# Threshold attention before two feed-forward layers on one core: weight conversions issued one at a time, and a pair's value products in four parts

## The chip, the cores and the metric

The kernel runs on one core of one Trainium2 chip. Its time is the device time of one launch in microseconds (us). A core has TensorE (PE in the profile, with its weight loads as PEld), VectorE (DVE), ScalarE (ACT), GpSimd (POOL), and SyncE (SP), which here issues the transfers between HBM and SBUF. Each engine works through its own list of instructions in order; a semaphore holds an instruction until what it needs on another engine is done.

## The reference

Attention over 4 x 8 heads of 576 rows and 64 columns, in which a row keeps only the scores within `tau` of its maximum, and then two feed-forward layers (512 to 1536 to 512 and 512 to 2048 to 512) over all 2304 tokens, in float32:

```python
scores = q @ k.T / sqrt(64)                     # per head, 576 x 576
scores = where(scores >= max(scores) - tau, scores, -1e9)
attn = exp(scores - max(scores)); attn /= sum(attn) + 1e-9
x = concat_heads(attn @ v)                      # 2304 x 512
x = (sigmoid(x @ w_gate) * (x @ w_val)) @ w_out
out = g(x @ w2_in) @ w2_out                     # g: piecewise quadratic
```

The weights reach the kernel as 64-bit floats, so the kernel has to turn them into float32 itself.

## The kernel before, in words

**Attention** goes over 16 pairs of heads (`p`), each in 5 steps (`u` = 0 to 4), 80 steps in all, numbered `t` = 5p + u. Below u0 to u4 are these steps. A step of u0 to u3 takes 128 query rows of both heads; u4 takes the 64 rows left over of each head, together in one tile. In a step four things happen that belong to different rows, as a pipeline written out by hand in the loop over `t` (L392 to L454):

- TensorE: `scores` of step t (L252, at u4 L248) into the PSUM tiles `wa` and `wb`; `turns` of step t-2 (L295 transposes the masked weights into PSUM tile `wt`, first those of one head and then of the other, and L296 transposes the left-over columns `lt`); a part of the products with the values (`attend`, L319) of the pair before.
- VectorE: `maxima` of step t (L261, one per head, reading `wa` and `wb`), then `masks` of step t-1 (L281, one per head; at u4 there is one row tile, so one of each).
- ScalarE: `copies` of step t-2 (L301 and L305, out of `wt` and `left`), `exponents` of step t (L273), `drain` (L329), which takes the value products out of the PSUM tile `av`.
- GpSimd: thresholds (L264), the copy of left-over columns `lt` behind each mask pair (L288), and the division by the row sums (L350).

`wa`, `wb`, `wt`, `left` and `av` exist once each, so the scores of the next step wait for the maxima of this one, and the transposes of one step for ScalarE's copies of the one before.

The value products of a pair are two rounds (`r` = 0, 1) of five column blocks `c` = 0 to 4; the table `rounds` (L386) says at which step which blocks are done. Block 4 uses the left-over columns (`rl`). `drain` follows in the step that does block 4.

**Work put into the attention steps.** `background` (L352) turns the first six weight blocks (groups `g`) into float32 while attention runs. A group is a transfer (`load_w`, L129), one ScalarE operation (`extract`, L145) and six VectorE operations (`convert`: L155, L157, L159, L161, L165, L169). The kernel takes one piece of it with `next(bg)`: at u0 of the pairs 1 to 12, ahead of the masks (L420), where a piece is three VectorE operations, and at u2 of the even pairs (L441), where it is the extract. Over the last three pairs the same place at u0 yields `"gap"` (L424) to the loop in `ffn` (L807), which then issues the VectorE halves of all `begun` splits into a high and a low float32r part (`split_xs`, L477, 768 columns; `split_list`, L192, 512 columns): two, two and three at one time. Their ScalarE halves are issued at the end of u4 before.

After attention the first layer starts with weight transfers, conversions and products of its own (`hidden`, `conversions`), all issued in program order behind the last attention steps.

Of the kernel before, what the change touches and what calls it, by code (L numbers as in the profile page):

```python
# [29 lines left out]
def kernel(  # L30
# [57 lines left out]
    high0 = const.tile([P, KD * P], F32, name="high0")  # L88
# [7 lines left out]
    w32 = {(0, 0, 0): ring[0], (0, 0, 1): ring[1]}  # L96
# [12 lines left out]
    def run(*gens):  # L109
        for g in gens:  # L110
            for _ in g:
                pass

    def load_w(ph, g):

        f, i = divmod(g, 3 - ph)
        ins, wo = ((w_gate, w_val), w_out) if ph == 0 else ((w2_in,), w2_out)
        if i < len(ins):
            src = ins[i][:, 2 * f * P : 2 * (f + 1) * P].rearrange("(k p) f -> p k f", p=P)
        else:  # L120
            src = wo[f * P : (f + 1) * P, :].rearrange("p (k f) -> p k f", k=KD)
        if ph == 0 and g < 6:
            t = early_raw[g % 2]
        else:
            n = 2 * KD * P
            t = pools["words"][:, pools["n"] % 6 * n :][:, :n]
            pools["n"] += 1
        r = t.bitcast(U32)
        nc.sync.dma_start(out=r.rearrange("p (k f) -> p k f", k=KD), in_=src)  # L129
        raws[ph, g] = r.rearrange("p (f w) -> p f w", w=2)  # L130
# [10 lines left out]
    def extract(ph, gs, c):  # L141

        n = KD * P
        for i, g in enumerate(gs):
            nc.scalar.activation(  # L145
                c[:, i * n : (i + 1) * n], raws[ph, g][:, :, 1].bitcast(F32), AF.Copy, scale=2.0**-112
            )

    def convert(ph, gs, c, a):


        n = KD * P
        c, a = c[:, : len(gs) * n], a[:, : len(gs) * n]
        cu, au = c.bitcast(U32), a.bitcast(U32)
        nc.vector.tensor_scalar(c, c, -DBL_TOP, DBL_TOP, op0=ALU.max, op1=ALU.min)  # L155
        yield
        nc.vector.tensor_scalar(au, cu, 3, None, op0=ALU.logical_shift_left)  # L157
        yield
        nc.vector.scalar_tensor_tensor(au, cu, 0x80000000, au, op0=ALU.bitwise_and, op1=ALU.bitwise_or)  # L159
        yield  # L160
        nc.vector.tensor_scalar(cu, au, 0xFF800000, None, op0=ALU.bitwise_and)  # L161
        yield
        for i, g in enumerate(gs):
            ci = c[:, i * n : (i + 1) * n]
            nc.vector.scalar_tensor_tensor(  # L165
                ci, raws.pop((ph, g))[:, :, 0], 2.0**-52, ci, op0=ALU.mult, op1=ALU.mult
            )
            yield
        nc.vector.tensor_tensor(a, a, c, op=ALU.add)  # L169
        yield  # L170
# [29 lines left out]
    def attention():  # L200
# [14 lines left out]
        U = nf + 1  # L215
        N = NP * U
# [73 lines left out]
        def turns(p, u):  # L290
            pr = pt.pop((p, u))
            for e in range(1 if u == nf else 2):
                for c in range(nf):
                    cs = slice(c * P, c * P + P)
                    nc.tensor.transpose(wt[:, e, cs], pr[:, e, cs], ident)  # L295
            nc.tensor.transpose(left[:, :P], lts.pop((p, u)).rearrange("p a b -> p (a b)"), ident)  # L296
# [34 lines left out]
        def denom(p):  # L331
            rs = sums[p % 2]
            nc.vector.reciprocal(rs, rs)
# [14 lines left out]
        def normalise(p, s):  # L348
            x, c = x_of(p), slice(s * HS, s * HS + HS)
            nc.gpsimd.tensor_tensor(x[:, c], x[:, c], rbs[:, p % 2 * S :][:, c], op=ALU.mult)  # L350

        def background():  # L352

            for g in range(2):
                load_w(0, g)
            yield
            for g in range(6):
                extract(0, (g,), high0)
                yield
                n = KD * P  # L360
                ops = convert(0, (g,), high0, w32[0, 0, g // 3][:, g % 3 * n : (g % 3 + 1) * n])
                run(itertools.islice(ops, 3))
                yield
                run(ops)
                if g + 2 < 6:
                    load_w(0, g + 2)
                yield

        def warm(n):

# [11 lines left out]
        warm(10)  # L382
        corner(0)
        bg = background()

        rounds = {5: (0, 0, 2), 6: (0, 2, 5), 7: (1, 0, 2), 8: (1, 2, 4), 9: (1, 4, 5)}  # L386
        final = {5: (0, 0, 5), 7: (1, 0, 5)}
        parts = {}
        for p in range(NP):
# [2 lines left out]
        for t in range(N + 9):  # L392
            p, u = divmod(t, U)
            on = t < N
            mk = divmod(t - 1, U) if 1 <= t <= N else None
            at = divmod(t - 2, U) if 2 <= t <= N + 1 else None

            pd, ud = divmod(t - U, U)
            pd2, ud2 = divmod(t - 2 * U, U)
            if ud2 in (2, 3) and 0 <= pd2 < NP:  # L400
                normalise(pd2, ud2 - 2)
            if on:
                scores(p, u)
            if t == N + 1:
                yield t - N, True
            if at:
                turns(*at)
            if ud == 2 and 0 <= pd < NP:
                nc.tensor.transpose(left[: 2 * nf + 1, P : 2 * P], sums[pd % 2], ident)
            for part in parts.get(t, ()):  # L410
                attend(*part)
            if on:
                maxima(p, u)
            if at:
                copies(*at)
            if on:
                exponents(p, u)
            if ud == 1 and 0 <= pd < NP:
                denom(pd)
            if on and u == 0 and p > 0:  # L420
                if p < 13:
                    next(bg, None)
                else:
                    yield t - N, "gap"  # L424
            if ud == 2 and 0 <= pd < NP:
                sum_rows(pd)
            for part in parts.get(t, ()):
                if part[2][-1] == nf:
                    drain(*part[:2])
            if mk:  # L430
                masks(*mk)
                if mk[1] == nf:
                    nc.gpsimd.tensor_scalar(sums[mk[0] % 2], sums[mk[0] % 2], 1e-9, None, op0=ALU.add)
            if on:
                if u == 1 and p + 1 < NP:
                    corner(p + 1)
                if u == 2 and p + 2 < NP:
                    load(p + 2)
                if u == 4 and p + 2 < NP:
                    load_v(p + 2)  # L440
                if t == 1 or u == 2 and p % 2 == 0 and p < 12:  # L441
                    next(bg, None)
            if ud == 3 and 0 <= pd < NP:
                spread(pd)
            if t == N - 1:
                wides[:] = [wb, wa, wt]
            if t == N:
                run(bg)
                nc.scalar.activation(dummy, half, AF.Sigmoid)
                st1.close()  # L450
            if t == N + 2:
                st2.close()
                ps_o.close()
            yield t - N, False  # L454

    def ffn(att):


        with ExitStack() as st:
# [340 lines left out]
                            up(0, 0, 0, n, i, pv[i], [kk])  # L800
                        yield

            early, taken, xops = {}, [], {}
            more = first_up()
            ahead = [split_xs(0, 0, 0, T, [c]) for c in range(KD)] + split_list(0, 0, 0, False)
            second = iter(())
            for step, free in att:  # L807
                if free == "gap":
                    for g in begun:
                        run(g)  # L810
                    continue
                if free:
                    late = sb("late", 1)
                    wins.append(late.tile([P, 4 * KD * P], F32R, name="win_1"))
                    wouts.extend(late.tile([P, 2, DM], F32R, name=f"wout_{i}") for i in (1, 2))
                    hp_ = sb("hp_", 2)
                    pools["words"] = cv("words", 1).tile([P, 12 * KD * P], F32, name="words")
                    pools["n"] = 0
                    for _, _, gs in todo[:2]:
                        for g in gs:  # L820
                            load_w(0, g)
                    continue
                if step in (-16, -11, -6):
                    begun, ahead = (ahead[:2], ahead[2:]) if step < -6 else (ahead, [])
                    for g in begun:
                        next(g)
                if step == 1:
                    second = split_parts(0, 0, 1, False)
                if step >= 0:
                    run(itertools.islice(second, 2))  # L830
                    run(itertools.islice(more, {0: 4, 1: 2, 2: 2}.get(step, 0)))
# [7 lines left out]
            n = 2 * KD * P  # L839
            slots = [wmore[:, i * n : (i + 1) * n] for i in range(4)] + [x[:, :n] for x in ring]  # L840
            n = 3 * KD * P
# [7 lines left out]
            for s in range(NS):  # L849
                nxt = order[s + 1] if s + 1 < NS else None  # L850
                ops = 8 if order[s][1] == 0 else 6
# [25 lines left out]
                _, t, f = order[s - 1]  # L877
# [74 lines left out]
```

## Time and profile before

| | us |
|---|---|
| median of three runs | 1143.96 |
| lowest and highest run | 1143.52, 1143.96 |
| the profiled execution, its own time | 1143.82 |
| its span, from the first to the last instruction | 1142.0 |
| TensorE busy in the span | 1109.9 (97%) |
| VectorE busy | 849.0 (74%) |
| ScalarE busy | 620.9 (54%) |
| GpSimd busy | 138.1 (12%) |

All durations below are from that one execution. Attention takes about the first 288 us of its span. A TensorE record ends by a model, and neighbouring records overlap by some hundredths of a us; where "idle before" stands behind a row, the engine did nothing in that time, and the name behind the arrow is what ended last before it went on.

### The profile page before, as it was taken

How to read it: one execution, taken by the hardware profiler on the slowest of the kernel's cores; microseconds unless marked ns; L12 is line 12 of the kernel's file. 1: busy time of each engine (PE TensorE's matmuls, PEld its weight loads, DVE VectorE, ACT ScalarE, POOL GpSimd, SP SyncE). 2: the span in 40 equal slices, each digit the busy share in tenths (PEclk: the TensorE clock that was granted, in tenths of full speed). 3: DMA queues.
4: the chain of work that ended last, by engine and by line, in shares of the span. 5: the costliest groups of instructions: out<-in, count | busy, mean ns of one | idle time of the engine just before them, and what ended most of it. 6: DMA issues, size and time to landing. Idle time of an engine off the chain costs nothing.

```text
span 1142.0 us, 17341 instructions
## 1 busy us (share of the span) xinstructions
PE 1109.9 (97%) x6372; PEld 944.5 (83%) x6372; DVE 849.0 (74%) x1484; ACT 620.9 (54%) x1048; POOL 138.1 (12%) x315
## 2 busy tenths in 40 slices
PE   8999999999799999999999999989999999999998
PEld 5555656556699999999999999988888888988887
DVE  6888888888499999767777762576677767676663
ACT  5777777787444344333344322366566655656553
POOL 3444544555100000000000000000000000000000
PEclk9999999999999999999999999999999999999999
DMA  4323233220665566455446524032312432143301
GB/s 131 88 76 89 78 81 78 62 71 21 212 205 177 176 199 231 168 183 178 154 161 212 176 78 162 19 111 86 133 67 104 156 121 97 72 161 114 111 20 55
DMA packets 65141, 139.09 MB, mean 122 GB/s; under 512 B 9616, under 2 KB 35872, under 8 KB 65056
## 3 DMA queue, kind: packets, MB, share of 16 engines
q1 hardware_dynamic: 64912, 137.98, 36.1%
q8 instruction: 50, 0.82, 0.3%
q14 instruction: 35, 0.29, 0.1%
q10 hardware_dynamic: 144, 0.00, 0.0%
HBM read 111.15 MB, written 26.81 MB: 121 GB/s over the span
## 4 chain that ended last, share of the span: by engine, by line
PE 85%; DVE 8%; ACT 3%; issue 2%; DMA 1%; SPq 0%; POOL 0%; DVEq 0%; POOLq 0%; ACTq 0%
PE y L743 15%; PE pu L610 14%; PE y L761 13%; PE pgv L486 8%; PE pgv L485 8%; PE pgv L487 8%; PE av L319 6%; PE w L295 5%; PE w L252 5%; DVE s L261 2%; PE w L248 2%; DVE p L281 1%; DVE high L165 1%; ACT sqs L619 1%; ACT sqs L620 1%
## 5 line engine op out<-in xcount | busy, mean ns | idle before, releaser
L485 PE MATMUL pgv<-xflat,win 128*128 128x384 f32 x560 | 188.5, 337 | 5.9 <-ACT act L541 3.8
L486 PE MATMUL pgv<-xflat,win 128*128 128x384 f32 x560 | 188.4, 336 | 0.1
L743 PE MATMUL y<-wout,hh 128*128 128x512 f32 x576 | 185.4, 397 | 3.0 <-ACT hh L628 3.0
L487 PE MATMUL pgv<-xflat,win 128*128 128x384 f32 x560 | 188.3, 336 | 0.0
L761 PE MATMUL y<-hh,wout 128*128 128x512 f32 (+1 forms) x576 | 146.7, 337 | 0.0
L261 DVE TENSOR_SCALAR_CACHE_REDUCE s<-w,nscale 128x576 f32<-128x576 f32 x144 | 112.7, 816 | 33.6 <-PE w L252 23.8
L743 PEld LDWEIGHTS y<-wout,hh 128*128 128x128 f32 x576 | 108.9, 189 | 28.0 <-ACT hh L628 3.3
L545 DVE TENSOR_TENSOR act<-pgv,act 128x384 f32<-128x384 f32 x70 | 38.9, 556 | 104.2 <-PE pgv L487 103.9
L743 PE MATMUL y<-wout,hl 128*128 128x512 f32 x288 | 114.3, 397 | 0.5 <-DVE hl L629 0.5
L485 PEld LDWEIGHTS pgv<-xflat,win 128*128 128x128 f32 x560 | 105.9, 189 | 7.9 <-ACT act L541 4.1
L281 DVE SCALAR_TENSOR_TENSOR p<-s,mx,ex 128x576 f32<-128x576 f32 x144 | 112.1, 812 | 0.5 <-POOL lt L288 0.5
L541 ACT ACTIVATE act<-pgv 128x384 f32<-128x384 f32 x70 | 34.2, 489 | 137.1 <-PE pgv L487 136.8
L273 ACT ACTIVATE ex<-s,mx 128x576 f32<-128x576 f32 x144 | 104.8, 775 | 7.2 <-DVE s L261 6.8
L486 PEld LDWEIGHTS pgv<-xflat,win 128*128 128x128 f32 x560 | 106.0, 189 | 2.0 <-DVE xflat L477 0.4
L761 PEld LDWEIGHTS y<-hh,wout 128*128 128x128 f32 x576 | 98.1, 188 | 11.3
L610 PE MATMUL pu<-xflat,win 128*128 128x384 f32 x576 | 105.1, 337 | 1.0 <-DVE sqs L689 0.7
L487 PEld LDWEIGHTS pgv<-xflat,win 128*128 128x128 f32 x560 | 106.0, 189 | 0.0
L546 ACT ACTIVATE hh<-act 128x384 fp32r<-128x384 f32 x72 | 38.0, 527 | 121.7 <-DVE act L545 121.3
L610 PEld LDWEIGHTS pu<-xflat,win 128*128 128x128 f32 x576 | 100.6, 188 | 2.4 <-DVE sqs L689 1.4
L295 PEld LDWEIGHTS w<-ident,p 128*128 128x128 f32 x576 | 62.8, 141 | 41.6 <-ACT ex L273 36.6
L761 PE MATMUL y<-hl,wout 128*128 128x512 f32 (+1 forms) x288 | 97.1, 337 | 0.0
L301 ACT ACTIVATE r<-w 128x1024 f32<-128x1024 f32 x64 | 65.7, 1026 | 49.7 <-PE w L295 49.6
(140 smaller groups left out, 1928.6 us busy)
## 6 DMA issues: line engine op xcount, KB each, us to landing
wmore<-saved SPq DMA_DIRECT2D x32, 512.0 KB
words<-in_moe_w_out_dram SPq DMA_DIRECT2D x26, 512.0 KB
tsum<-tsaved SPq DMA_DIRECT2D x24, 512.0 KB
wmore<-saved SPq DMA_DIRECT2D x15, 768.0 KB
words<-in_moe_w_in_dram SPq DMA_DIRECT2D x16, 512.0 KB
saved<-w SPq DMA_DIRECT2D x16, 512.0 KB
w<-saved SPq DMA_DIRECT2D x16, 512.0 KB
w<-saved SPq DMA_DIRECT2D x9, 768.0 KB
```

Source lines behind the costliest of these rows:

```text
L261: nc.vector.tensor_scalar(t[:, e], w[:, :, :HS], nscale, None, op0=ALU.mult, op1=ALU.min, accum_out=mx[:, 0, e : e + 1])
L273: nc.scalar.activation(ex[:, e], t[:, e], AF.Exp, scale=-1.0, bias=mx[:, 0, e : e + 1])
L281: nc.vector.scalar_tensor_tensor(pr[:, e], t[:, e].rearrange("p a b -> p (a b)"), mx[:, 1, e : e + 1], ex[:, e].rearrange("p a b -> p (a b ...
L295: nc.tensor.transpose(wt[:, e, cs], pr[:, e, cs], ident)
L301: nc.scalar.activation(rt[r].rearrange("p e c n -> p (e c) n")[:, :, o : o + P], wt.rearrange("p e (c n) -> p (e c) n", n=P), AF.Copy,)
L319: nc.tensor.matmul(av[e * D : e * D + D, :n], vs[p % 3][:, e, c], rt[r][:, e, c] if c < nf else rl[r], start=c == 0, stop=c == nf,)
L485: nc.tensor.matmul(ps, ih[:, i, kk], xh[:, kk, c], start=(kk == 0), stop=False)
L486: nc.tensor.matmul(ps, ih[:, i, kk], xl[:, kk, c], start=False, stop=False)
L487: nc.tensor.matmul(ps, il[:, i, kk], xh[:, kk, c], start=False, stop=(kk == KD - 1))
L610: nc.tensor.matmul(ps[bank], l[:, k], r[:, k], start=bool(new) and k == m == 0, stop=k == HK - 1 and m == 2, skip_group_check=True,)
L743: nc.tensor.matmul(y[b], l[:, ts_], r, start=first and m == 0, stop=last and m == 2)
L761: nc.tensor.matmul(at(y, a, b), l[:, ds_], r[:, c], start=new and m == 0, stop=last and m == 2, skip_group_check=True,)
```

## The change

Three edits. The six operations of `convert` become six pieces, taken one at a time behind the masks at u0, u2 and u3 of each pair, from step 3 to step 62; the place at u0 ahead of the masks goes. (The extra piece at u2 of even pairs stays, so there a VectorE operation and an extract come together.) From step 63 on the same three places yield `"gap"`, which now issues one split instead of all. And the last block of the second round of value products moves from u4 to u3, its `drain` with it.

```diff
-                ops = convert(0, (g,), high0, w32[0, 0, g // 3][:, g % 3 * n : (g % 3 + 1) * n])
-                run(itertools.islice(ops, 3))
-                yield
-                run(ops)
+                yield from convert(0, (g,), high0, w32[0, 0, g // 3][:, g % 3 * n : (g % 3 + 1) * n])
                 if g + 2 < 6:
                     load_w(0, g + 2)
-                yield
...
-        rounds = {5: (0, 0, 2), 6: (0, 2, 5), 7: (1, 0, 2), 8: (1, 2, 4), 9: (1, 4, 5)}
+        rounds = {5: (0, 0, 2), 6: (0, 2, 5), 7: (1, 0, 2), 8: (1, 2, 5)}
...
-            if on and u == 0 and p > 0:
-                if p < 13:
-                    next(bg, None)
-                else:
-                    yield t - N, "gap"
...
                 masks(*mk)
...
+            if on and u in (0, 2, 3) and t > 2:
+                if t <= 12 * U + 2:
+                    next(bg, None)
+                else:
+                    yield t - N, "gap"
...
                 if free == "gap":
-                    for g in begun:
-                        run(g)
+                    run(*begun[:1])
+                    del begun[:1]
                     continue
```

On TensorE, from u3 of a pair over u4 to u0 of the next (`w_126` and `w_127` are `wa` and `wb`, `w_128` is `wt`):

```order
 L319 MATMUL av<-r_161,v_164 64x320 x4
+L319 MATMUL av<-rl_163,v_164 64x320 x2
 L248 MATMUL w_126<-qk,corner_75 128x288 x2
 L295 MATMUL w_128<-ident,p 128x128 x8
 L296 MATMUL left<-ident,lt 128x128
-L319 MATMUL av<-rl_163,v_164 64x320 x2
 L252 MATMUL w_126<-qk 128x288
 L252 MATMUL w_127<-qk 128x288
```

Two products (four records in the trace) moved from behind u4's transposes to ahead of its scores, so that nothing stands between those transposes and the scores of the next pair.

On VectorE, the end of a pair and u0 of the next, before (`s` and `mx` are the outputs of the maxima, `p` of the masks, `high_84` and `w_0_82` the tiles of a conversion):

```order
L261 TENSOR_SCALAR s,mx_77<-w_126,nscale 128x576
L281 SCALAR_TENSOR_TENSOR p,sum_81<-s,mx_76,ex 128x576 x2
L261 TENSOR_SCALAR s,mx_76<-w_126,nscale 128x576
L261 TENSOR_SCALAR s,mx_76<-w_127,nscale 128x576
L161 TENSOR_SCALAR high_84<-w_0_82 128x512
L165 SCALAR_TENSOR_TENSOR high_84<-raw_86,high_84 128x512
L169 TENSOR_TENSOR w_0_82<-w_0_82,high_84 128x512
L281 SCALAR_TENSOR_TENSOR p,sum_81<-s,mx_77,ex 128x576
```

Three operations of a conversion stand between u0's maxima and the one mask of u4.

The same engine with the change, from u2's masks of an even pair to u0 of the next:

```order
L281 SCALAR_TENSOR_TENSOR p,sum_80<-s,mx_77,ex 128x576 x2
L169 TENSOR_TENSOR w_0_82<-w_0_82,high_84 128x512
L261 TENSOR_SCALAR s,mx_77<-w_126,nscale 128x576
L261 TENSOR_SCALAR s,mx_77<-w_127,nscale 128x576
L281 SCALAR_TENSOR_TENSOR p,sum_80<-s,mx_76,ex 128x576 x2
L155 TENSOR_SCALAR high_84<-high_84 128x512
L261 TENSOR_SCALAR s,mx_76<-w_126,nscale 128x576
L281 SCALAR_TENSOR_TENSOR p,sum_80<-s,mx_77,ex 128x576 x2
L261 TENSOR_SCALAR s,mx_77<-w_126,nscale 128x576
L261 TENSOR_SCALAR s,mx_77<-w_127,nscale 128x576
L281 SCALAR_TENSOR_TENSOR p,sum_80<-s,mx_76,ex 128x576
L157 TENSOR_SCALAR w_0_82<-high_84 128x512
```

One operation now stands behind the masks at u2, u3 and u0, none at u4 and u1, and u4's mask comes right behind u0's maxima.

## Rows read from the trace of the kernel before

**Rows 1.** From 100 to 150 us: PE, PEld, DVE, ACT, POOL busy; clock, DMA share, GB/s.

```profile
100.00:150.00 50.00, 47.41 (x336) 29.48 (x336) 44.03 (x114) 36.47 (x69) 23.66 (x53) 1.00 0.35 92
```

**Rows 2.** Waits of TensorE's products, 20 to 285 us: total us, times, longest us.

```profile
PE w L295 <- DVE p L281: 10.1, 12, 1.0
PE w L295 <- ACT ex L273: 2.8, 3, 1.0
```

**Rows 3.** Timeline (start us, us, instruction, [idle before]): TensorE, u0 to next u0.

```profile
125.77 1.24 PE L252 MATMUL w<-qk 64*128 64x288 f32 x8
...
129.09 1.24 PE L252 MATMUL w<-qk 64*128 64x288 f32 x8
131.02 0.63 PE L295 MATMUL w<-ident,p 128*128 128x128 f32 x4 [0.68 <-DVE p L281]
...
133.13 1.24 PE L252 MATMUL w<-qk 64*128 64x288 f32 x8
...
136.77 1.24 PE L252 MATMUL w<-qk 64*128 64x288 f32 x8
...
140.30 1.24 PE L248 MATMUL w<-qk,corner 128*128 128x288 f32 x4
141.38 1.04 PE L295 MATMUL w<-ident,p 128*128 128x128 f32 x8
...
142.45 0.76 PE L319 MATMUL av<-rl,v 128*64 128x320 f32 x4
143.14 1.24 PE L252 MATMUL w<-qk 64*128 64x288 f32 x8
144.31 1.09 PE L295 MATMUL w<-ident,p 128*128 128x128 f32 x8
```

**Rows 4.** Timeline of VectorE over the same pair: u0 and u1, then u4.

```profile
128.53 0.42 DVE L155 TENSOR_SCALAR high<-high 128x512 f32<-128x512 f32 x1
...
129.44 0.69 DVE L159 SCALAR_TENSOR_TENSOR w<-high,w 128x512 uint32<-128x512 uint32 x1
130.05 0.81 DVE L281 SCALAR_TENSOR_TENSOR p<-s,mx,ex 128x576 f32<-128x576 f32 x1
...
131.00 0.82 DVE L261 TENSOR_SCALAR_CACHE_REDUCE s<-w,nscale 128x576 f32<-128x576 f32 x1
...
141.58 0.82 DVE L261 TENSOR_SCALAR_CACHE_REDUCE s<-w,nscale 128x576 f32<-128x576 f32 x1 [0.49 <-PE w L248]
...
142.32 0.81 DVE L281 SCALAR_TENSOR_TENSOR p<-s,mx,ex 128x576 f32<-128x576 f32 x1
```

**Rows 5.** The two splits of one gap in the last pairs, VectorE.

```profile
251.15 1.82 DVE L477 TENSOR_TENSOR xflat<-xall,xflat 128x768 fp32r<-128x768 f32 x2
```

**Rows 6.** Pair 0, u4 and the next u0: masks, transposes, maxima, scores.

```profile
18.63 0.81 DVE L281 SCALAR_TENSOR_TENSOR p<-s,mx,ex 128x576 f32<-128x576 f32 x1
18.83 0.42 PEld L295 LDWEIGHTS w<-ident,p 128*128 128x128 f32 x4 [0.76 <-ACT rl L305]
...
19.51 0.42 PEld L295 LDWEIGHTS w<-ident,p 128*128 128x128 f32 x4 [0.26 <-DVE p L281]
19.58 0.82 DVE L261 TENSOR_SCALAR_CACHE_REDUCE s<-w,nscale 128x576 f32<-128x576 f32 x1
...
20.46 1.24 PE L252 MATMUL w<-qk 64*128 64x288 f32 x8 [0.19 <-DVE s L261]
```

**Rows 7.** The last u4 and the step behind it: ScalarE's copy, then TensorE's transposes.

```profile
282.94 1.03 ACT L301 ACTIVATE r<-w 128x1024 f32<-128x1024 f32 x1 [0.86 <-PE w L295]
284.02 1.09 PE L295 MATMUL w<-ident,p 128*128 128x128 f32 x8 [0.32 <-ACT r L301]
```

**Rows 8.** GpSimd at u1: two thresholds, the second beside a mask, then the left-over copy.

```profile
131.99 0.28 POOL L264 TENSOR_SCALAR mx<-mx,tau_b 128x1 f32<-128x1 f32 x1 [0.35 <-DVE s L261]
132.66 0.85 POOL L264 TENSOR_SCALAR mx<-mx,tau_b 128x1 f32<-128x1 f32 x1 [0.38 <-DVE s L261]
...
134.25 0.29 POOL L288 COPY lt<-p 128x128 f32<-128x128 f32 x1 [0.73 <-DVE p L281]
```

More of the change, by code (lines that the diff above doesn't have):

```diff
@@ L801, in first_up @@
                         yield
-            early, taken, xops = {}, [], {}
+            early, taken, xops, begun = {}, [], {}, []
             more = first_up()
```

## The prediction

> **What bounds the kernel now.** I read the busy shares first, by stretch. Over most of attention TensorE works 47.41 of 50 us and VectorE 44.03, at a granted clock of 1.00 [rows 1]. So TensorE sets the pace, some 5% of its time is idle, and VectorE has little to spare. The clock is at its upper level (2.4 GHz) with these idles in it, so their removal gives none back.
>
> Next, the waits of TensorE's products: they are nearly all one wait, the transposes L295 for the masks L281, 12 times and 10.1 us in all, and three more of 2.8 us put down to ScalarE [rows 2]. That is 12.9 us in 15 places, one a pair.
>
> Then the timeline of one pair, to see where. From one first score product to the next, u0 takes 3.32 us, u1 4.04, u2 3.64, u3 3.53 and u4 2.84 [rows 3]: 17.37 us a pair. The wait lies in u1, here 0.68 us. VectorE shows why: at u0 three conversion operations run from 128.53 to 130.05, ahead of the one mask of u4, which ends at 130.86 [rows 4]; the transposes of u1 need that mask. In every second pair the three are the longer ones (rows like L159 with 0.69 us instead of L155's 0.42), hence waits of up to 1.0. In the last three pairs two splits of 1.82 us stand in the same place [rows 5]; I take their waits as the mask's too, though the releaser named is ScalarE's.
>
> **The change, term by term.** Times in a step count from its first score product; maxima start 1.28 behind that when VectorE is free (140.30 to 141.58 [rows 3, 4]). Maxima and masks follow each other every 0.74 us (141.58, 142.32) and last 0.82. Behind a second mask the next maxima start at the earliest 0.95 after that mask's start (130.05 to 131.00 [rows 4]).
>
> *Removed:* the 15 waits, -12.9 us, as u4's mask now comes right behind u0's maxima.
>
> *The operations behind masks.* There are 36 conversion operations, half of them of L155's size and half of L159's [rows 4], and 7 splits. None ran behind a mask before, so each costs between nothing and its length (0.42 to 0.69; a split of two in 1.82, 0.91). Step by step, with the longest that stands there:
> - u0: maxima at 1.55 (see below) and 2.29, mask 3.03 to 3.85, operation to about 4.5. The next maxima are due at 3.32 + 1.28 = 4.60. Hidden.
> - u1, without its wait 3.36 long: no operation. Maxima 1.28, 2.02, reciprocal, masks to 4.4; the transposes of the second head that need them come at 3.36 + 1.17 + 0.42 = 4.95. Hidden.
> - u2: masks end at 4.33, operation to about 4.95 (L169, in even pairs). The next maxima are due at 3.64 + 1.28 = 4.92. Late by 0.03, with a split by 0.25.
> - u3 is now longer by the moved products, 142.45 to 143.14 or 0.69 [rows 3], so 4.22. Masks end at 4.33, operation to 4.75 (L155 or L161, both short), next maxima due at 5.50. Hidden, and u2's lateness ends here.
>
> So I take nothing for them in pairs 1 to 15. The cover is VectorE's idle time ahead of the maxima, 0.49 in rows 4. The extract that comes with L169 at u2 of even pairs runs on ScalarE behind u2's exponentials; its transfer moves on SP's queue from ahead of that step's loads of q and k to behind them, ten steps before its use. Neither is waited for.
>
> In pair 0, VectorE is what TensorE waits for: u4's maxima start at 19.58, right behind the masks that end at 19.44, and the scores at 20.46 wait for them [rows 6]. An operation put between is paid, 0.42 less the 0.14 that was idle: +0.3 (between 0 and 0.4).
>
> *The moved products.* TensorE's work is the same. But u4 shrinks from 2.84 to 2.15, and three things can be late there:
> - The next scores need `wa`, so u4's maxima: 1.28 + 0.82 = 2.10, and 0.06 until TensorE goes (20.40 to 20.46 [rows 6]): 2.16 against 2.15.
> - u3's masks start at 2.02 and 2.76 and end at 2.84 and 3.58. u0's transposes start at 2.16 + 1.17 = 3.33. They go head by head: in pair 0 the first four loads ran at 18.83, ahead of the second mask's end, and the other four at 19.51, 0.07 behind it [rows 6]. The first half needs 2.84; the second is due 0.42 later, at 3.75, over 3.65. On time.
> - `wt` must be empty: ScalarE's L301 of 1.03 us starts where the moved products stood, 2.15, and TensorE goes 0.05 behind it [rows 7]: 3.23 against 3.33.
>
> ScalarE's drain moves with the products, into its 0.86 us of idle time ahead of L301 [rows 7]. So the step holds with margins of 0.1 us. I take 0.02 a pair, 14 pairs, +0.3. Bounds: 0, and 0.35 a pair (transposes held for both masks, 3.65 + 0.03 - 3.33), 4.9 us.
>
> u0's maxima also come later, at 1.55 in place of 1.28, since the second mask started at 2.76 (2.76 + 0.95 - 2.16); that is in the list above.
>
> Behind the last u4 there are no scores. There the transposes wait for L301 already, 0.32 us, with the products in between [rows 7]. Those leave, L301 does not come sooner, and u4 starts 0.69 later: +0.7.
>
> *Sum:* -12.9 + 0.3 + 0.3 + 0.7 = -11.6. The profiled execution took 1143.82, which gives 1132.2; the median is 0.14 above it, so **1132.4 us**. What follows attention is issued in order behind it, its transfers too, and shifts as a whole.
>
> **A rule against it.** A GpSimd threshold takes 0.28 us beside maxima and 0.85 beside a mask [rows 8]: GpSimd is held up by a VectorE operation with two SBUF inputs. The copy `lt` (0.29 [rows 8]) follows a mask pair at once; now a conversion can hold it. At u0 it would end near 4.5 + 0.29 = 4.8 and release L296 at 4.9; L296 is due behind four transposes, 3.32 + 1.17 + 0.42 = 4.91. The Trainium skill, "SBUF — State Buffer", section "SBUF: two separate sides", says that GpSimd and a VectorE operation of that kind take the shared port pair in turn, whole instructions long, which agrees with the 0.85. By it the sum would be the same, or 0.6 more where that is missed by 0.1 in the six even pairs: 1133.0.
>
> **Rivals.**
> 1. *The wait moves to u4 and u0.* The margins there are 0.01 to 0.1 us, and if transposes are held for both masks each pair pays 0.35: 1132.4 + 4.9 = 1137.3. For it: VectorE is 88% busy. Against: the two halves in rows 6.
> 2. *`lt` comes late*, as the rule has it: 1133.0. For it the 0.85; against it, 4.9 is still in time.
> 3. *Nothing gained.* u4 is so short that masks, `lt` and copy together bring back 0.8 a pair, 15 times, about 12 us: 1144.4. Against: each alone is in time above.
> 4. *Slower: VectorE becomes the bound.* Each operation behind masks delays the next maxima and through them the scores. Fully paid, six groups of three short operations (0.42) and three long ones (0.69), 20.0, and four splits of 0.91 and three of 0.69, 5.7, give 25.7 less the 0.3 counted for pair 0: 1157.8. It decides from 11.6 / 43 = 0.27 us an operation. Against: 0.49 idle ahead of the maxima, and scores that wait 1 us behind them.
>
> **The chances.** My forecast, 1130.9 to 1134, 0.75; rival 2 lies in it, 0.05 more; rival 1 0.10; rival 3 0.05; rival 4 0.05. The range starts at all added costs zero (1143.96 - 12.9 = 1131.1, with 0.2 for the runs' own spread), and ends past rival 1 at 1137.5, since the forecast alone leaves out more than I may. A measurement can tell 0.2%, 2.3 us, from no change. Faster by more: 0.90; within it: 0.05; slower: 0.05.
>
> **What would show it.** Right: no wait of L295 for L281 at u1; 16.7 us from pair to pair in place of 17.4; VectorE's idle before maxima gone at u2 and u0 but left at u3's end; TensorE near 49.9 of 50 us busy. Wrong: a wait of L295 or L252 at each u0 (rival 1), of L296 at u1 (rival 2), or scores waiting for maxima behind conversions (rival 4).

## The result and the profile after

The changed kernel takes 1128.39 us (1127.83 to 1129.2, four runs) against 1143.96 (1143.52 to 1148.13, four runs): a ratio of 0.9856, 95% interval 0.9832 to 0.988. That is 15.6 us less. The forecast was 11.6 less, and the range began at 1130.9, above the result. The waits went as forecast; a gain in TensorE's own work, which the forecast put at nothing, came on top.

The stretch of the profile after that answers to [rows 1] (PE, PEld, DVE, ACT, POOL busy, clock, DMA share, GB/s):

```profile
100.00:150.00 50.00, 50.00 (x360) 31.44 (x356) 46.29 (x123) 39.91 (x76) 30.48 (x58) 1.00 0.32 87
```

TensorE is busy for all of the 50 us. All that is left of the waits of its products from 20 to 270 us, where [rows 2] had 12.9 us:

```profile
PE w L295 <- ACT r L301: 1.0, 1, 1.0
PE w L252 <- DVE s L261: 0.3, 1, 0.3
```

The first is the one behind the last u4, 0.32 before and 1.00 now, the second the one in pair 0, 0.19 before and 0.26 now. The timeline of TensorE over one pair, from u1 to the next u1, as in [rows 3]:

```profile
122.48 1.24 PE L252 MATMUL w<-qk 64*128 64x288 f32 x8
...
125.79 1.24 PE L252 MATMUL w<-qk 64*128 64x288 f32 x8
...
129.43 1.24 PE L252 MATMUL w<-qk 64*128 64x288 f32 x8
...
131.74 1.30 PE L319 MATMUL av<-r,v 128*64 128x320 f32 x8
132.86 0.71 PE L319 MATMUL av<-rl,v 128*64 128x320 f32 x4
133.50 1.24 PE L248 MATMUL w<-qk,corner 128*128 128x288 f32 x4
134.58 1.04 PE L295 MATMUL w<-ident,p 128*128 128x128 f32 x8
135.45 0.27 PE L296 MATMUL left<-ident,lt 128*128 128x128 f32 x1
135.66 1.24 PE L252 MATMUL w<-qk 64*128 64x288 f32 x8
...
138.98 1.24 PE L252 MATMUL w<-qk 64*128 64x288 f32 x8
```

u1 takes 3.31 us, u2 3.64, u3 4.07, u4 2.16 and u0 3.32: 16.50 a pair. Before it was 17.64 and 17.37 in turn, and without the waits 16.69. The forecast for u4 was 2.16, and for u3 4.22. The 0.15 between 4.22 and 4.07 is what was missed.

VectorE in the same pair (the mask of u4 and the operation behind it at u0, then u2 and u3), as in [rows 4]:

```profile
122.19 0.81 DVE L281 SCALAR_TENSOR_TENSOR p<-s,mx,ex 128x576 f32<-128x576 f32 x1
122.93 0.42 DVE L157 TENSOR_SCALAR w<-high 128x512 uint32<-128x512 uint32 x1
123.75 0.82 DVE L261 TENSOR_SCALAR_CACHE_REDUCE s<-w,nscale 128x576 f32<-128x576 f32 x1 [0.40 <-PE w L252]
...
129.28 0.82 DVE L281 SCALAR_TENSOR_TENSOR p<-s,mx,ex 128x576 f32<-128x576 f32 x1
130.03 0.68 DVE L159 SCALAR_TENSOR_TENSOR w<-high,w 128x512 uint32<-128x512 uint32 x1
130.71 0.82 DVE L261 TENSOR_SCALAR_CACHE_REDUCE s<-w,nscale 128x576 f32<-128x576 f32 x1
...
133.67 0.42 DVE L161 TENSOR_SCALAR high<-w 128x512 uint32<-128x512 uint32 x1
134.78 0.82 DVE L261 TENSOR_SCALAR_CACHE_REDUCE s<-w,nscale 128x576 f32<-128x576 f32 x1 [0.69 <-PE w L248]
```

The maxima behind u2's operation start 1.28 us behind their scores (129.43 to 130.71), without idle time ahead of them; behind u0's and u3's operations 0.40 and 0.69 are left.

Two of the last pairs take 16.65 us instead of 16.50, and the reason is the copy `lt`, behind a split at u0. GpSimd and VectorE there:

```profile
221.44 1.51 POOL L264 TENSOR_SCALAR mx<-mx,tau_b 128x1 f32<-128x1 f32 x1 [0.45 <-DVE s L261]
...
221.93 0.95 DVE L473 TENSOR_TENSOR xflat<-xall,xflat 128x768 fp32r<-128x768 f32 x1
...
222.90 0.28 POOL L288 COPY lt<-p 128x128 f32<-128x128 f32 x1
```

The transposes of u1 on TensorE, in the pair above and here:

```profile
123.65 0.66 PE L295 MATMUL w<-ident,p 128*128 128x128 f32 x4
124.14 0.27 PE L296 MATMUL left<-ident,lt 128*128 128x128 f32 x1
...
222.65 0.66 PE L295 MATMUL w<-ident,p 128*128 128x128 f32 x4
223.24 0.33 PE L296 MATMUL left<-ident,lt 128*128 128x128 f32 x1
```

The threshold takes 1.51 us beside u4's mask and the split behind it, so the copy ends at 223.18 and L296 comes 0.59 behind the transposes' start instead of 0.49. No wait row shows this, since the records of TensorE overlap there.

### The profile page after: what moved, and what is told of

The parts are those of the page before. It is cut to its first block, busy times and chain, and to the rows that moved or that the text cites. A ratio compares the mean times of both kernels' runs of the same rounds, so it can differ in the third digit from the quotient of the medians.

```text
span 1127.1 us, 17344 instructions
## 1 busy us (share of the span) xinstructions
PE 1108.3 (98%) x6372; PEld 946.5 (84%) x6372; DVE 845.5 (75%) x1484; ACT 621.5 (55%) x1048; POOL 161.1 (14%) x315
## 4 chain that ended last, share of the span: by engine, by line
PE 91%; DVE 4%; ACT 2%; issue 1%; POOL 0%; DVEq 0%; POOLq 0%; ACTq 0%
PE y L739 15%; PE pu L606 14%; PE y L757 13%; PE pgv L482 8%; PE pgv L481 8%; PE pgv L483 8%; PE av L319 8%; PE w L252 7%; PE w L295 6%; PE w L248 2%; PE left L296 1%; ACT sqs L615 1%; ACT sqs L616 1%; ACT hh L624 1%; PE av L368 0%
## 5 line engine op out<-in xcount | busy, mean ns | idle before, releaser
L264 POOL TENSOR_SCALAR mx<-mx,tau_b 128x1 f32<-128x1 f32 x144 | 98.1, 685 | 68.3 <-DVE s L261 68.2
```

The lines of the kernel that those rows point to most:

```text
L264: nc.gpsimd.tensor_scalar(mx[:, 1, e : e + 1], mx[:, 0, e : e + 1], tau_b, None, op0=ALU.add)
```

## The experiments

Seven kernels were run, each timed in five rounds beside the kernel before (1143.6 to 1143.7 in these). To tell a tenth of a us a pair apart, the distance between the u4 scores L248 of neighbouring pairs is read from each trace; away from the first and the last pairs it is the same to 0.01 us (to 0.03 in the second round in one step; the kernels with waits at u1 alternate between two values).

| kernel | median us | ratio to before, 95% | us a pair |
|---|---|---|---|
| before | 1143.96 | | 17.37, 17.64 |
| changed | 1128.39 | 0.9856 (0.9832, 0.988) | 16.50 |
| conversions and splits alone | 1130.74 | 0.9887 (0.9874, 0.9901) | 16.65 |
| value products alone | 1144.79 | 1.0016 (1.0007, 1.0025) | 17.51, 17.77 |
| left-over transpose between | 1133.71 | 0.9914 (0.9901, 0.9928) | 16.80 |
| splits of the last pairs as before | 1131.46 | 0.9904 (0.9889, 0.9919) | 16.50 |
| value products between scores and transposes | 1133.01 | 0.9908 (0.9894, 0.9922) | 16.80 |
| second round in one step | 1137.95 | 0.995 (0.9937, 0.9962) | 17.16 to 17.19 |
| both ends mended | 1127.84 | 0.9861 (0.9846, 0.9876) | 16.50 |

**Each edit alone.** First the changed kernel with the table of five groups:

```diff
-        rounds = {5: (0, 0, 2), 6: (0, 2, 5), 7: (1, 0, 2), 8: (1, 2, 5)}
+        rounds = {5: (0, 0, 2), 6: (0, 2, 5), 7: (1, 0, 2), 8: (1, 2, 4), 9: (1, 4, 5)}
```

> The conversions and splits one at a time behind the masks, with the value products in five groups as before. Theory A (every run of value products between other TensorE work costs a fixed 0.15 us beside some 0.13 us a product, so that the four groups save TensorE time): the pairs take 16.65 us instead of 16.50, 15 times, 2.3 us more than the changed kernel, less 0.7 for the last pair, where the short u4 cost that: about 1130.0, and no wait of L295 for L281. Theory B (the move of the products is free, and all the gain is the waits): pairs of 16.50 here too, 0.7 us less than the changed kernel, 1127.7.

It took 1130.74, with pairs of 16.65 us and no wait at u1; the wait behind the last u4 is 0.3 again. So the conversions carry some 13 of the 15.6 us, and the moved products a gain of their own of 0.15 us a pair: theory A, not B. The pairs are also 0.04 shorter than the 16.69 that the kernel before had beside its waits. So a wait cost here 0.04 us more than the idle time that stands behind its row.

Then the kernel before with the table of four groups, and nothing else:

> The four groups alone, conversions and splits three (two) at a time ahead of u4's mask as before. Theory A with the masks as the bound: TensorE's work falls by 0.15 us a pair, but the shorter u4 moves u0's maxima from 1.28 to 1.55 us behind u0's scores and the mask of u4 with them, so the wait at u1 grows from 0.7 to 0.95 us to 1.0 to 1.2; with 0.7 us lost behind the last pair the time is 1144 to 1146.5, no better than before. Theory C (the two edits add up, each worth the same alone): 15 times 0.15 less and 0.7 more, 1142.3.

It took 1144.79, 0.16% over before. Its waits:

```profile
PE w L295 <- DVE p L281: 13.2, 12, 1.2
PE w L295 <- ACT ex L273: 3.6, 3, 1.3
PE w L295 <- ACT r L301: 1.0, 1, 1.0
```

The waits for the mask grew from 10.1 and 2.8 us to 13.2 and 3.6. A shorter u4 puts u0's scores earlier, but u0's maxima have to wait for the mask pair in front of them, so u4's mask comes later against the scores. TensorE's saving and 0.13 us a pair more go into the wait. The moved products are worth something only once the mask no longer waits for conversions.

**Where the 0.15 us come from.** In the changed kernel the left-over transpose of u3 was put between the products of blocks 2 and 3 and those of block 4:

```diff
+                if late_left and cs_[0] == 2:
+                    attend(p_, r_, cs_[:2])
+                    turn_left(*at)
+                    late_left = False
+                    attend(p_, r_, cs_[2:])
```

> The changed kernel, but in u3 the left-over transpose L296 is issued between the products of blocks 2 and 3 and those of block 4, so that the 12 products of u3 are two groups again and nothing else moves to another step. Theory A: 0.15 us more in each of 15 pairs, pairs of 16.65 us, 1130.7. Theory B (a group costs nothing; the pairs got shorter because u4 got shorter): pairs of 16.50, 1128.4.

The pairs became 16.80 us, 0.30 more. Theory B falls, as the steps were left as they were; theory A has the right sign and half the size. The timeline of u3:

```profile
148.77 1.09 PE L295 MATMUL w<-ident,p 128*128 128x128 f32 x8
149.80 1.30 PE L323 MATMUL av<-r,v 128*64 128x320 f32 x8
151.03 0.33 PE L300 MATMUL left<-ident,lt 128*128 128x128 f32 x1
151.28 0.76 PE L323 MATMUL av<-rl,v 128*64 128x320 f32 x4
151.97 1.24 PE L248 MATMUL w<-qk,corner 128*128 128x288 f32 x4
```

Line numbers moved by four. The transpose takes 0.25 from start to start where it took 0.21 behind other transposes, and the four products 0.69 again, as in [rows 3], while in the changed kernel behind eight others they took 0.64 (132.86 to 133.50), both with the way into the next scores. The group adds two passages, into the products' weights of 128*64 and back to 128*128. TensorE's weight loads of the kernel before show a passage itself:

```profile
139.07 0.74 PEld L319 LDWEIGHTS av<-r,v 128*64 128x64 f32 x8 [0.17 <-issue]
140.30 0.78 PEld L248 LDWEIGHTS w<-qk,corner 128*128 128x128 f32 x4 [0.49 <-issue]
141.14 1.04 PEld L295 LDWEIGHTS w<-ident,p 128*128 128x128 f32 x8
```

From L248 to L295, both 128*128, the first weights of L295 load at 141.14, while L248 still runs (the products start at 141.38). From L319 to L248 the shape changes, and the weights load only when the product starts, at 140.30. So theory A was made sharper: 0.15 us at each change of the weights' shape (A1), or at each change from one kind of product to another (A2). The products of block 4 between u4's scores L248 and the transposes, both 128*128, tell them apart:

```diff
+            if u == nf:
+                for part in parts.pop(t, ()):
+                    attend(*part)
             if at:
                 turns(*at)
```

> The changed kernel with the products of block 4 at u4 again, but between u4's scores L248 and the transposes L295. Scores of u4, transposes and left-over transposes all have weights of one shape (128*128), the value products 128*64, the scores of u0 to u3 64*128. Theory A1 (a fixed 0.15 us at each change of the shape of the weights, since the next weights are then not loaded ahead): u3's group is still there, and the new one adds two changes of shape, so pairs of 16.80 us, as with the left-over transpose between, 1132.5 to 1133.5. Theory A2 (0.15 us at each change from one kind of product to another, whatever the shapes): scores to transposes was a change already, so one more, pairs of 16.65, 1130.7.

Pairs of 16.80 us and 1133.01: A1. The kernel with five groups alone had one change of shape more than the changed kernel (into the products and out to L252's 64*128, where the changed kernel goes from transposes to L252 at once) and 0.15 us more; these two have two more and 0.30. The printed shape alone is not the rule: the transpose of the row sums (L405) has weights of 128*9, and they are loaded ahead behind weights of 128*128. In the changed kernel:

```profile
127.78 0.14 PEld L296 LDWEIGHTS left<-ident,lt 128*128 128x128 f32 x1
127.89 0.09 PEld L405 LDWEIGHTS left<-ident,sum 128*9 128x9 f32 x1
...
128.00 0.27 PE L405 MATMUL left<-ident,sum 128*9 128x128 f32 x1
```

L405 starts 0.11 us behind L296 (127.89), as transposes of one shape do. So the 0.15 is shown for changes between 128*128, 128*64 and 64*128, and no others. That TensorE has nothing loaded ahead across such a change was read from the rows; why, no run shows. The Trainium skill, "TensorEngine Tiling (Array Packing)", section "Tiling Modes", says that changing the tiling mode drains TensorE, and gives no price; the traces agree so far as no weights are loaded ahead across these changes, at 0.15 us each.

**The last three pairs.** The changed kernel with `run(*begun)` ahead of u4's mask at u0, as before:

> The changed kernel with the splits of the last three pairs two, two and three at one time ahead of u4's mask at u0, as before; the conversions stay one at a time. If the three waits put down to ScalarE were the mask's behind the splits: they come back with 0.9 to 1.3 us each, 2.7 to 3.9 us more, 1131.1 to 1132.3. Rival: they were ScalarE's own (its halves of the splits hold up its copies and exponentials), and those are issued where they were in the changed kernel too, so nothing changes, 1128.4.

It took 1131.46, 3.1 more, and the waits are back under the same name:

```profile
PE w L295 <- ACT ex L273: 3.6, 3, 1.2
```

ScalarE's halves of the splits are where they were in the changed kernel, so the three waits were the mask's, behind VectorE's splits, whatever releaser the row names. They are 0.3 us longer each than before, since u4 is short, as in the kernel with the products alone.

**Fewer groups still.** With a change of shape at 0.15 us, three groups should be better than four. The second round was put whole into u3:

```diff
-        rounds = {5: (0, 0, 2), 6: (0, 2, 5), 7: (1, 0, 2), 8: (1, 2, 5)}
+        rounds = {5: (0, 0, 2), 6: (0, 2, 5), 8: (1, 0, 5)}
```

> The changed kernel with the second round's products all in u3: three groups a pair, none at u2. By the cost of changes alone one change less, 16.35 us a pair, 1126.1. But u2 would then be some 2.45 us long, and the scores of u3 need the second of u2's maxima, which ends at 1.28 + 0.74 + 0.82 + 0.06 = 2.90: theory D (a step of two heads cannot be shorter than 2.90 us) has a wait of L252 for L261 of 0.3 to 0.5 us a pair, pairs of 16.7 to 16.85, 1131 to 1134.

1137.95, pairs of some 17.17 us: theory D's direction, and more than its size. u2 to u3 on TensorE, and GpSimd beside it:

```profile
112.12 1.24 PE L252 MATMUL w<-qk 64*128 64x288 f32 x8
...
114.54 1.71 PE L252 MATMUL w<-qk 64*128 64x288 f32 x8
116.18 1.09 PE L295 MATMUL w<-ident,p 128*128 128x128 f32 x8
117.39 0.33 PE L296 MATMUL left<-ident,lt 128*128 128x128 f32 x1
```

```profile
115.04 2.07 POOL L264 TENSOR_SCALAR mx<-mx,tau_b 128x1 f32<-128x1 f32 x2
117.06 0.28 POOL L288 COPY lt<-p 128x128 f32<-128x128 f32 x1
```

u2 is 2.42 us long. The scores of u3 then take 1.64 to the transposes in place of 1.17: within them TensorE stands at the second head's products until u2's second maxima are done (114.14 to 114.96 on VectorE), and the record spans that, so no wait of L252 shows. This is the 0.47 of theory D. Then the left-over transpose comes 1.21 behind the transposes' start, 0.28 more than the usual 0.93: its copy `lt` ran only at 117.06, behind two thresholds that took 2.07 us and VectorE's L169. With 0.15 saved, 16.50 - 0.15 + 0.47 + 0.28 is 17.10 of the 17.17, and the left-over transpose itself takes 0.06 more (0.26 to the products in place of 0.20). The late `lt` is rival 2's mechanism, in a kernel that leaves it no room.

**Both ends mended.** Pair 14 keeps its block 4 at u4, and the conversions begin at step 5:

```diff
-            for i, (r, a, b) in (rounds if p + 1 < NP else final).items():
+            for i, (r, a, b) in (five if p + 2 == NP else rounds if p + 1 < NP else final).items():
...
-            if on and u in (0, 2, 3) and t > 2:
-                if t <= 12 * U + 2:
+            if on and u in (0, 2, 3) and t > 3:
+                if t <= 12 * U + 3:
```

> The changed kernel with its two ends mended: pair 14 keeps its block 4 at u4 (the last u4, behind which no scores stand), and the conversions begin at step 5 instead of 3 and end at step 63. That puts L165 and L169 together at u2 of the even pairs, 1.3 us behind the masks. If the terms hold: 0.7 us less at the last u4 (its wait 0.3 instead of 1.0), 0.1 to 0.3 less in pair 0, and the two operations at u2 make u3's maxima late by 0.6, which u3's length takes up: pairs still 16.50, 1127.5. Rival (VectorE has no such room): waits at u3, u4 or u0 in every second pair of 0.2 to 0.7 us, 1129 to 1132.

The pairs stay at 16.50, the wait behind the last u4 is 0.3, and that in pair 0 is 0.2 in place of 0.3. The span is 1126.3 against 1127.1. The median, 1127.84, is below the changed kernel's 1128.39, but the runs overlap (1127.64 to 1128.06, and 1127.83 to 1129.2), and the ratios to the kernel before are alike (0.9861 and 0.9856). The times show no gain; the trace shows the two waits shorter, by 0.7 and 0.1 us. The two operations at u2 of an even pair:

```profile
146.16 0.69 DVE L165 SCALAR_TENSOR_TENSOR high<-raw,high 128x512 f32<-128x512 uint32 x1
146.89 0.81 DVE L169 TENSOR_TENSOR w<-w,high 128x512 f32<-128x512 f32 x1
147.62 0.81 DVE L261 TENSOR_SCALAR_CACHE_REDUCE s<-w,nscale 128x576 f32<-128x576 f32 x1
...
150.92 0.82 DVE L261 TENSOR_SCALAR_CACHE_REDUCE s<-w,nscale 128x576 f32<-128x576 f32 x1 [0.27 <-PE w L248]
```

u3's maxima are late, and u4's have 0.27 us of idle time ahead of them all the same: the lateness ends in u3, and TensorE does not see it.

## Why the prediction was right, and where it was wrong

- *The 15 waits, -12.9.* Right. They are gone, and the kernel with the conversions and splits alone has the gain.
- *Operations behind masks at nothing.* Right for the 35 conversions behind pair 0, at u0, u2 and u3, also with two of them at u2. Not right for two of the seven splits: the list took a conversion as the longest operation at u0, but in the last pairs a split of 0.95 us stands there, and twice it cost 0.15.
- *Pair 0, +0.3.* Some 0.1: from the second score products to pair 1's took 12.05 us (8.11 to 20.16) in place of 11.93.
- *The step from u4 to u0.* Worked out to 2.16 us and measured 2.16, without a wait. The 0.02 a pair that I added for its thin margins was not needed (0.3 in all). Rival 1 did not come.
- *Behind the last u4, +0.7.* Right: 1.00 for 0.32.
- *The rule on the shared port (rival 2).* GpSimd's copy did come later where a conversion follows the masks, but L296 did not come late for it there. Behind the two splits at u0 it did, by 0.10 us. The second round in one step shows it in every pair, where u2 is short.
- ***The moved products: "TensorE's work is the same"*** is the step that failed, and with it the bound below of that term, which I put at zero and so ruled out a gain. The number of products is the same, but two changes of weight shape, into the group at u4 and out of it, became one. That is 0.15 us in each of 15 pairs, 2.3 us. The figures stood in the trace of before: four products took 0.69 us at u4, eight took 1.22 at u3 (139.08 to 140.30, row below the list). The difference is 0.53 for four, so a group has 0.16 that does not go with its products. I took the 0.69 whole from one step to the other.
- *The wait as its idle time alone.* Without it a pair is 0.04 us shorter still, 0.6 in all, which the row's idle time does not hold.

The eight products at u3 in the kernel before; the scores L248 follow at 140.30 [rows 3]:

```profile
139.08 1.30 PE L319 MATMUL av<-r,v 128*64 128x320 f32 x8
```

In the two profiled executions the spans differ by 14.9 us against the 11.6 worked out: 2.3 for the changes of shape, 0.6 for the waits' ends, 0.5 not paid at u4 and in pair 0 make 15.0. The rest is small: the first u4 scores came 0.4 earlier in the execution after (16.88 for 17.29; the seven kernels scatter there from 16.3 to 17.5), and two of the last pairs took 0.15 more than 16.50, behind their splits.

## What to carry to other kernels

When an engine works without a gap, moving its instructions is not free of price or gain: read what a group of n and of 2n of them takes from start to start, and charge the fixed part to every group that is made or joined. An edit that is worth nothing alone may be worth something once another has taken the wait away, and the shorter step may make the old wait longer, so the two have to be costed together. For a wait that an operation causes in front of a mask, look for the place behind the mask where the engine idles anyway; here the idle time ahead of the maxima held operations of up to 0.69 us, and two of them where the next step was long. A split of 0.95 us at u0 was too much, not for the maxima but for GpSimd's small copy beside it.

## What the hardware showed that was not expected

A change of the weight shape between neighbouring products, among 128*128, 128*64 and 64*128, cost TensorE 0.15 us each, in three kernels with one, two and two such changes a pair more than the changed one (16.65, 16.80 and 16.80 us for 16.50). Each of these figures holds changes in both directions; a single direction was not measured. Between unlike products of one shape the next weights were loaded ahead, and so were those of 128*9 behind 128*128. And a wait inside a run of score products shows in no wait row, only in the record's length: 1.71 us for 1.24. GpSimd's threshold, 0.28 us beside maxima, took 1.51 beside a mask and a split that followed it at once.
